# The second dense product of 23 token tiles by Strassen's seven half-size products, in a fused Fourier mixer and feed-forward kernel

## The chip, the cores and the metric

The kernel runs on one core of one Trainium2 chip. TensorE multiplies matrices and leaves the results in PSUM, in 8 banks of 512 f32 per partition; VectorE (DVE) and ScalarE (ACT) read PSUM and write SBUF; GpSimd (POOL) does some elementwise work and issues the DMAs of its own queue; SyncE (SP) issues the other DMAs. The metric is device time in microseconds, as the median of several runs.

## The reference

The input x has 8 batches of 3008 tokens by 256 features. First a Fourier mixer, then a feed-forward layer over all 24064 tokens:

```python
X = np.fft.rfft(x, axis=1)
Yr = Xr @ w_r - Xi @ w_i + b_r
Yi = Xr @ w_i + Xi @ w_r + b_i
# soft threshold of both at 0.01, then
y = np.fft.irfft(Y, n=3008, axis=1)

h = y @ w_in                  # 256 -> 2048
r = np.maximum(h, 0.0)
g = s * (r * r) + b
out = g @ w_out               # 2048 -> 256
```

The kernel computes in f16 with f32 sums. It multiplies r*r by w_out and applies s and b afterwards: out = s * (r*r @ w_out) + bias, where bias is b times the column sums of w_out.

## The kernel before

**Tiles and slots.** The feed-forward layer runs over 48 token tiles in a fixed order (`_tile_order`, L73): six "wide" tiles for each of batches 0 and 1 (512, 512 and 480 tokens, twice), then five "main" tiles of 512 for each later batch, and six "tail" tiles (512 or 384 tokens) made of the leftover tokens of two batches. The batches begin at tiles 0, 6, 12, 17, 23, 29, 35 and 41; the 384-token tails are tiles 28, 40 and 44. Each tile has 16 slots, one for each block `mc` of 128 hidden features. The main loop (L911 to L920) goes over tiles and slots. In slot `mc` of tile `ti` it writes down, in this order:

- the Fourier units that `plan` has for this slot,
- the first product of block `mc` of tile `ti` (`first_mm`, L768): two matmuls of up to 512 columns. They go to the two-bank PSUM tile `psh`, of which there are two. After each odd block one relu on ScalarE (L788) takes both banks to `rt` in SBUF (f32), and one square takes `rt` to `gt` (f16), on ScalarE (L792) or VectorE (L795). I call the squares of a tile k = 0 to 7; square k is written down in slot 2k + 1,
- a sixteenth of the second product of the tile before (`second_mms`, L837): for each of four groups of 128 tokens, 16 matmuls with a piece of `gt` as stationary operand and 256 columns of `w_out_t` as moving operand (L852), four per slot. Two groups share one PSUM bank (`psa`, two banks). After two groups one VectorE instruction (L862) applies s and the bias and writes `ost`, which SP stores.

**The Fourier units.** Batch 0 is transformed at the start (`first_batch`). The later ones go in small units spread over the slots of earlier tiles by `schedule` (L875 to L908): `s1_units` (a 94-point transform, whose result goes to DRAM and comes back in another layout), `s23_units` (the 32-point transform, the mixing, the threshold, the inverse transform, and DRAM again) and `s4_units` (the last 94-point transform, which writes `yt`). For a batch that begins at tile m, `s4_units` run in the last 14 slots before tile m, `s1_units` of the next batch end 8 slots before it, and `s23_units` of the next batch begin in its third slot.

**Who takes what.** `load` keeps a running sum of estimated microseconds for ScalarE and VectorE. PSUM evacuations (`evac`, L165) and the squares (L791) go to the engine with the lower sum; the fixed work of both engines is added where it is written down.

**Order in a queue.** The code only writes the instructions down. The framework under it puts each engine's instructions in an order of its own, by priority and by when it expects their inputs, and adds the waits for data and for buffers. A buffer pool with n buffers hands the same memory out again every n tiles, once all readers of the old tile are done.

Of the kernel before, what the change touches and what calls it, by code (L numbers as in the profile page):

```python
# [96 lines left out]
def kernel(  # L97
# [50 lines left out]
    dpool = ctx.enter_context(tc.tile_pool(name="dram", bufs=2, space=bass.MemoryType.DRAM))  # L148
    xpool = ctx.enter_context(tc.tile_pool(name="xp", bufs=4))
    upool = ctx.enter_context(tc.tile_pool(name="up", bufs=3))  # L150
    uspool = ctx.enter_context(tc.tile_pool(name="usp", bufs=5))
    xfpool = ctx.enter_context(tc.tile_pool(name="xfp", bufs=4))
    mpool = ctx.enter_context(tc.tile_pool(name="mp", bufs=2))
# [4 lines left out]
    rpool = ctx.enter_context(tc.tile_pool(name="rp", bufs=3))  # L158
    gpool = ctx.enter_context(tc.tile_pool(name="gp", bufs=15))
    opool = ctx.enter_context(tc.tile_pool(name="op", bufs=3))  # L160


    load = {"act": 0.0, "dve": 0.0}

    def evac(dst, src, cols, scale=None):  # L165
        ta, td = 0.17 + cols / 1200.0, 0.15 + cols / 960.0
        if load["act"] + ta <= load["dve"] + td:
            load["act"] += ta
            if scale is None:
                return None, nc.scalar.copy(out=dst, in_=src)  # L170
            return None, nc.scalar.mul(out=dst, in_=src, mul=scale)
        load["dve"] += td
        if scale is None:
            return nc.vector.tensor_copy(out=dst, in_=src), None
        return nc.vector.tensor_scalar_mul(out=dst, in0=src, scalar1=scale), None
# [24 lines left out]

    XCH = 8
    x16 = {}

    def emit_load_x(b, first=None):
        xv = x[b].rearrange("(n1 n2) d -> n1 (n2 d)", n2=N2)
        for c in range(N2 // XCH):
            t = xpool.tile([P, XCH * D], F16, name="x16", tag="x16")
            if first is not None:
                gate = nc.gpsimd.tensor_copy(out=t[0:1, 0:1], in_=first)
            parts = 2 if b == 0 else 1  # L210
            w = XCH * D // parts
            for i in range(parts):
                nc.gpsimd.dma_start(  # L213
                    out=t[0:N1, i * w : (i + 1) * w],
                    in_=xv[:, c * XCH * D + i * w : c * XCH * D + (i + 1) * w],
                )
            x16[(b, c)] = t
# [21 lines left out]

    b_g = cpool.tile([P, 2, D], F32, name="b_g")  # L240
    nc.vector.memset(b_g, 0.0)
# [4 lines left out]
    F_2 = [uspool.tile([P, H, P], F16, name="F_2", tag="us") for _ in range(2)]  # L246
    b_h = cpool.tile([P, D], F16, name="b_h")
    nc.vector.memset(b_h, 0.0)

    for i, bv in enumerate((b_r, b_i)):  # L250
        nc.gpsimd.dma_start(out=b_h[64 * i : 64 * i + 1], in_=bv.unsqueeze(0))
    sel_t = cpool.tile([P, P], F16, name="sel_t")
    eye_t = cpool.tile([P, P], F16, name="eye_t")
    C_t = cpool.tile([96, 96], F16, name="C_t")
# [83 lines left out]

    w_sum = cpool.tile([P, 2, D], F16, name="w_sum")

# [8 lines left out]
    def make_bias():  # L349
        ps = other_bank()  # L350
        for i in range(2):
            nc.tensor.matmul(ps[:, 0:D], ones, w_sum[:, i], start=(i == 0), stop=(i == 1))
        nc.scalar.activation(out=bias_bc, in_=ps[:, 0:D], func=AF.Copy, scale=bb_bc)

    us = {}
# [216 lines left out]
    def s1_units(b, more_banks=False):  # L572

        ud = dpool.tile([96, N2, D], F16, name="ud", tag="ud")
        hold = {}

        def unit(i):
            c, j = divmod(2 * i, XCH)
            if j == 0:
                hold["u"] = upool.tile([P, XCH, D], F16, name="u", tag="u")  # L580
            ps = any_bank() if more_banks else one_bank()
            nc.tensor.matmul(  # L582
                ps[0:96, :], A_t[0:N1, :], x16[(b, c)][0:N1, j * D : (j + 2) * D],
                start=True, stop=True,
            )
            u = hold["u"]
            evac(u[0:96, j : j + 2, :], ps[0:96, :].rearrange("p (j d) -> p j d", j=2), 512)
            if j == XCH - 2:
                nc.sync.dma_start(
                    out=ud[:, c * XCH : (c + 1) * XCH, :], in_=u[0:96]  # L590
                )
            if i == N2 // 2 - 1:
                uv = ud.rearrange("k n d -> (k n) d").rearrange("(q p) d -> p q d", p=P)
                for q in range(4):
                    t = uspool.tile([P, 6, D], F16, name="us", tag="us")
                    nc.sync.dma_start(out=t, in_=uv[:, 6 * q : 6 * q + 6, :])
                    us[(b, q)] = t

        return [lambda i=i: unit(i) for i in range(N2 // 2)]

    def s23_units(b):
# [8 lines left out]
        def fwd_unit(i):  # L610
# [13 lines left out]
            nc.vector.tensor_tensor(out=xt[:, 0], in0=xt[:, 1], in1=xt[:, 2], op=ALU.add)  # L624
            load["dve"] += 0.25
            xf[i] = xt

        def sum_unit(h):

            ps = one_bank().rearrange("p (i e) -> p i e", i=2)  # L630
            for i in range(2):
                for dc in range(DC):
                    nc.tensor.matmul(  # L633
                        ps[:, i, :], xf[2 * h + i][:, 0, dc], W_t[:, dc, 0],
                        start=(dc == 0), stop=(dc == DC - 1),
                    )
            s = mpool.tile([P, 2, D], F32, name="s", tag="m")
            nc.scalar.copy(out=s, in_=ps)
            load["act"] += 0.6
            hold[h] = s  # L640

        def mix_unit(i):
# [16 lines left out]
            nc.vector.tensor_tensor(out=t, in0=t, in1=m, op=ALU.subtract)  # L659
            load["dve"] += 1.75  # L660

# [53 lines left out]
    def s4_units(b):  # L715
# [6 lines left out]
        def unit(g):  # L722
# [5 lines left out]
            for j in range(w):  # L728
                h, k = divmod(n2 + j, HW)
                nc.tensor.matmul(  # L730
                    ps[:, j * 96 : (j + 1) * 96],
                    vs[(b, h)][:, k, ec * P : (ec + 1) * P], C_t,
                    start=True, stop=True,
                )
            evac(
                yt[:, ec, n2 : n2 + w, :],
                ps[:, 0 : w * 96].rearrange("p (j n) -> p j n", n=96), w * 96,
            )
# [27 lines left out]
    hold_h = {}  # L766

    def first_mm(ti, mc):  # L768
        tl = tiles[ti]
# [18 lines left out]
        nc.scalar.activation(out=rt[:, :, 0:w], in_=ps[:, :, 0:w], func=AF.Relu)  # L788
        gt = gpool.tile([P, 2, 512], F16, name="gt", tag="gt")
        load["act"] += 0.17 + w / 600.0  # L790
        if load["act"] + 0.25 + w / 600.0 < load["dve"]:  # L791
            nc.scalar.activation(out=gt[:, :, 0:w], in_=rt[:, :, 0:w], func=AF.Square)  # L792
            load["act"] += 0.25 + w / 600.0
        else:
            nc.vector.tensor_tensor(  # L795
                out=gt[:, :, 0:w], in0=rt[:, :, 0:w], in1=rt[:, :, 0:w], op=ALU.mult
            )
            load["dve"] += 0.15 + w / 480.0
        gts[(ti, mc // 2)] = gt

    def store(tl, sub, src):
# [35 lines left out]
    def second_mms(ti):  # L837

        tl = tiles[ti]
        w = width(tl)  # L840
        size = sub_size(tl)
        nsub = -(-w // size)
        hold = {}

        def mm(sub, mc):
# [3 lines left out]
            if h == 0 and mc == 0:  # L849
                hold["ps"] = other_bank().rearrange("p (h e) -> p h e", h=2)  # L850
            ps = hold["ps"]
            nc.tensor.matmul(  # L852
                ps[0:size, h, :], gts[(ti, mc // 2)][:, mc % 2, sub * size : (sub + 1) * size],
                w_out_t[:, mc, :],
                start=(mc == 0), stop=(mc == MC - 1),
            )
            if sub == nsub - 1 and mc % 2 == 1:
                gts.pop((ti, mc // 2))
            if mc == MC - 1 and (alone or h == 1 or sub == nsub - 1):
# [5 lines left out]
                )  # L865
                load["dve"] += 0.12 + 0.27 * k
                for i in range(k):
                    store(tl, sub - k + 1 + i, ost[:, i, :])

        return [lambda s=s, m=m: mm(s, m) for s in range(nsub) for m in range(MC)]  # L870


    plan = {}
# [10 lines left out]
    )  # L884
    load.update(act=0.0, dve=0.0)
    def load_x_2():
        emit_load_x(2, us[(1, 3)][0:1, 0, 0:1])

# [7 lines left out]
    plan.setdefault(14, []).append(make_bias)  # L896
    plan.setdefault(18, []).append(load_x_2)
    schedule(24, 42, s23_units(1))
    schedule(mark[1] - 12, 16, s4_units(1))
    for b in range(2, B):  # L900
# [6 lines left out]
        if b + 1 < B:  # L907
            plan.setdefault(s1 + 6, []).append(lambda b=b: emit_load_x(b + 1))  # L908

    ti_n = len(tiles)  # L910
    for ti in range(ti_n + 1):  # L911
        nxt = second_mms(ti - 1) if ti else []
        per_slot = -(-len(nxt) // MC)
        for mc in range(MC):
            if ti < ti_n:
                for u in plan.pop(ti * MC + mc, []):
                    u()
                first_mm(ti, mc)
            for u in nxt[mc * per_slot : (mc + 1) * per_slot]:
                u()  # L920
# [31 lines left out]
```

## Time and profile before

| what | before |
|---|---|
| median of 3 runs | 846.99 us (846.75 to 849.01) |
| span of the profiled execution, first to last instruction | 844.6 us |
| busy in the span: TensorE, its weight loads, VectorE, ScalarE | 835.1, 601.3, 694.7, 640.6 us |
| second product (L852): matmuls | 3024 |
| first product (L781): matmuls | 1536 |
| relu (L788), squares on VectorE (L795), squares on ScalarE (L792) | 384, 319, 65 |
| moved by DMA | 96.06 MB, 114 GB/s on average |

The median is of runs that were timed as a whole; the span is of one other execution, taken with the profiler, and counts from its first to its last instruction. Busy times are sums of instruction durations. Instructions on one engine overlap a little, matmuls much, so a busy share near 100% on TensorE does not yet say that it is at its peak pace; for that one looks at when consecutive matmuls start.

### The profile page before, as it was taken

The page shows a single profiled execution, that of the slowest core. Times are in us where ns is not written, and L with a number is a line of the kernel's source. Part 1 is how long each engine was busy: PE and PEld are TensorE (multiplying, and loading weights), DVE is VectorE, ACT ScalarE, POOL GpSimd, SP SyncE. Part 2 cuts the span into 40 slices and gives each one's busy share as a digit, 9 for nine tenths or more (in the row PEclk, how much of TensorE's full clock was granted, in tenths as well). Part 3 has the DMA queues.
Part 4 walks back from the last instruction along what each step waited for, and adds up shares of the span by engine and source line. Part 5 has one row for each costly group of instructions (what it writes and reads, how often), then busy time and mean ns, then how long its engine had stood idle before and what let it go on. Part 6 is the DMA issues. An engine that isn't in the chain of part 4 may idle for free.

```text
span 844.6 us, 17119 instructions
## 1 busy us (share of the span) xinstructions
PE 835.1 (99%) x6654; PEld 601.3 (71%) x6654; DVE 694.7 (82%) x1034; ACT 640.6 (76%) x862; POOL 45.9 (5%) x73
## 2 busy tenths in 40 slices
PE   8999999999999999999999999999999999999998
PEld 7857767777677766777677776777667777766765
DVE  5999987888888988888888888798978888776674
ACT  5987887778778877788777787778877778666673
POOL 4630000000000001000000000000000000000000
PEclk9999999999999999999999999999999999999999
DMA  7955467224851367324761247613354223411111
GB/s 200 181 151 118 119 161 199 74 77 98 202 156 54 103 171 188 93 70 107 189 174 50 81 101 196 172 43 90 106 152 125 59 78 97 113 33 38 38 44 50
DMA packets 105939, 96.06 MB, mean 114 GB/s; under 512 B 9607, under 2 KB 97675, under 8 KB 104515
## 3 DMA queue, kind: packets, MB, share of 16 engines
q1 hardware_dynamic: 99362, 80.55, 32.9%
q0 software_dynamic: 6496, 14.42, 10.6%
q8 instruction: 52, 0.85, 0.4%
q14 instruction: 29, 0.23, 0.1%
HBM read 53.52 MB, written 46.66 MB: 119 GB/s over the span
## 4 chain that ended last, share of the span: by engine, by line
PE 92%; ACT 3%; DVE 2%; DMA 1%; issue 1%; POOL 0%; DVEq 0%; ACTq 0%; POOLq 0%
PE psa L852 38%; PE psh L781 37%; PE psf L647 4%; PE psf L582 3%; PE psf L633 2%; PE psf L677 2%; PE psf L618 2%; PE psf L730 2%; ACT rt L788 1%; DMA x<-in_x_dram 1%; PE psm L425 1%; POOL x L213 0%; ACT yt L170 0%; DVE z L463 0%; PE psf L456 0%
## 5 line engine op out<-in xcount | busy, mean ns | idle before, releaser
L788 ACT ACTIVATE rt<-psh 128x1024 f32<-128x1024 f32 (+2 forms) x384 | 387.2, 1009 | 120.2 <-PE psh L781 118.8
L795 DVE TENSOR_TENSOR gt<-rt 128x1024 f16<-128x1024 f32 (+2 forms) x319 | 382.3, 1202 | 94.4 <-ACT rt L788 93.4
L852 PE MATMUL psa<-w_out_t,gt 128*128 128x256 f16 (+1 forms) x3024 | 454.4, 272 | 0.1
L852 PEld LDWEIGHTS <-gt 128*128 128x128 f16 (+1 forms) x3024 | 300.9, 101 | 186.6 <-issue 1.1
L781 PE MATMUL psh<-yt,w_in 128*128 128x512 f16 (+1 forms) x1344 | 396.8, 378 | 0.2 <-ACT rt L788 0.2
L781 PEld LDWEIGHTS <-w_in 128*128 128x128 f16 x1536 | 142.7, 98 | 26.2 <-issue 1.2
L862 DVE SCALAR_TENSOR_TENSOR ost<-psa,s_bc,bias_bc 128x512 f32<-128x512 f32 (+2 forms) x97 | 71.1, 733 | 9.6 <-PE psa L852 7.9
L792 ACT ACTIVATE gt<-rt 128x1024 f16<-128x1024 f32 (+2 forms) x65 | 68.2, 1050 | 0.9
L652 DVE TENSOR_TENSOR ring<-psf,s 128x512 f16<-128x512 f32 x84 | 57.6, 685 | 3.3 <-PE psf L647 3.2
L170 ACT CAST v<-psf 128x512 f16<-128x512 f32 x77 | 44.8, 582 | 19.4 <-PE psf L677 19.4
L170 ACT CAST xf<-psf 128x512 f16<-128x512 f32 x79 | 46.3, 586 | 8.8 <-PE psf L618 8.8
L781 PE MATMUL psh<-tail,w_in 128*128 128x512 f16 (+1 forms) x192 | 52.1, 353 | 0.0
L170 ACT CAST u<-psf 96x512 f16<-96x512 f32 x74 | 42.8, 580 | 11.2 <-PE psf L582 10.9
L647 PE MATMUL psf<-W_g,xf 128*128 128x256 f16 x336 | 50.4, 273 | 0.0
L170 ACT CAST yt<-psf 128x480 f16<-128x480 f32 (+2 forms) x76 | 39.0, 520 | 14.7 <-PE psf L730 14.2
L213 POOL DMA_DIRECT2D x<-in_x_dram x36 | 18.8, 527 | 432.9 <-PE psf L582 431.7
L582 PE MATMUL psf<-x,A_t 94*96 94x512 f16 x102 | 38.9, 382 | 1.0 <-ACT yt L170 0.6
L658 DVE TENSOR_TENSOR ring<-ring,high 128x512 f16<-128x512 f16 x84 | 35.6, 423 | 2.3
L659 DVE TENSOR_TENSOR ring<-ring 128x512 f16<-128x512 f16 x84 | 35.6, 423 | 2.1
L657 DVE TENSOR_TENSOR ring<-ring,low 128x512 f16<-128x512 f16 x84 | 35.5, 422 | 1.6
L647 PEld LDWEIGHTS <-xf 128*128 128x128 f16 x336 | 32.9, 98 | 4.1 <-issue 0.2
L730 PE MATMUL psf<-C_t,vs 96*128 96x96 f16 x448 | 33.2, 205 | 0.0
(100 smaller groups left out, 508.6 us busy)
## 6 DMA issues: line engine op xcount, KB each, us to landing
out_dram<-ost SPq DMA_DIRECT2D x152, 128.0 KB
ud<-u SPq DMA_DIRECT2D x28, 384.0 KB
us<-ud SPq DMA_DIRECT2D x28, 384.0 KB
vd<-v SPq DMA_DIRECT2D x42, 256.0 KB
vs<-vd SPq DMA_DIRECT2D x14, 768.0 KB
x<-in_x_dram POOLq DMA_DIRECT2D x28, 376.0 KB, 6.3
ring<-ring SPq DMA_DIRECT2D x280, 32.0 KB
out_dram<-ost SPq DMA_DIRECT2D x16, 120.0 KB
```

Source lines behind the costliest of these rows:

```text
L170: return None, nc.scalar.copy(out=dst, in_=src)
L582: nc.tensor.matmul(ps[0:96, :], A_t[0:N1, :], x16[(b, c)][0:N1, j * D : (j + 2) * D], start=True, stop=True,)
L647: nc.tensor.matmul(ps[:, r, :], xt[:, 2 - r, dc], W_g[:, dc, r], start=(dc == 0), stop=(dc == DC - 1),)
L652: nc.vector.tensor_tensor(out=t, in0=ps, in1=hold[i // 2][:, i % 2].unsqueeze(1).to_broadcast([P, 2, D]), op=ALU.add,)
L658: nc.vector.tensor_tensor(out=m, in0=m, in1=high, op=ALU.min)
L730: nc.tensor.matmul(ps[:, j * 96 : (j + 1) * 96], vs[(b, h)][:, k, ec * P : (ec + 1) * P], C_t, start=True, stop=True,)
L781: nc.tensor.matmul(o, w_in_t[dc][:, mc * P : (mc + 1) * P], r, start=(dc == 0), stop=(dc == DC - 1),)
L788: nc.scalar.activation(out=rt[:, :, 0:w], in_=ps[:, :, 0:w], func=AF.Relu)
L792: nc.scalar.activation(out=gt[:, :, 0:w], in_=rt[:, :, 0:w], func=AF.Square)
L795: nc.vector.tensor_tensor(out=gt[:, :, 0:w], in0=rt[:, :, 0:w], in1=rt[:, :, 0:w], op=ALU.mult)
L852: nc.tensor.matmul(ps[0:size, h, :], gts[(ti, mc // 2)][:, mc % 2, sub * size : (sub + 1) * size], w_out_t[:, mc, :], start=(mc == 0), sto ...
L862: nc.vector.scalar_tensor_tensor(out=ost[0:size, 0:k], in0=ps[0:size, 0:k], scalar=s_bc[0:size], in1=bias_bc[0:size].unsqueeze(1).to_broad ...
```

## The change

For 23 of the 48 tiles, `seven_mms` takes the place of `second_mms`. The 512 (or 480) tokens are cut in two halves i, the 16 hidden blocks into even and odd blocks k, and the 256 output columns into halves. With A(i,k) the squared activations and B(k,j) blocks of w_out, the product of 2 x 2 blocks is done with seven products of blocks instead of eight, by Winograd's form of Strassen's method: S1 = A21 + A22, S3 = A11 - A21, S2 = A11 - S1 (kept with the sign turned where that is handier), S4 = A12 + S2, and four combinations of w_out blocks (T), computed once on POOL. S1, S3 and S2 are f16 sums on VectorE, in two halves q each; S4 is a DMA from POOL's queue that adds A11 (by then S2) onto A12 in SBUF. A product n is for j in two token groups, 8 blocks c: matmuls of 128 columns. Two products share a bank, so a tile fills four groups of banks in turn, and `leave(group)` combines the finished products on VectorE with s and the bias.

`gt` becomes a larger tile that holds four squares of both halves (4 buffers of it instead of 15 of the small ones). The planner's prices are set anew: the fixed part of each (`over`) falls from 0.17 and 0.15 to 0.07 and 0.07 once the main loop begins, and the price of a relu and of both kinds of square likewise. The last 94-point transform computes 94 columns, not 96. To make room in SBUF, several pools change: x has 3 buffers and one apart (it was 4), `u` has 5 of half the size (3), `us` 4 (5), `xf` 3 (4), and small constants share memory with later tiles. The fourth chunk of each x is loaded later (slot 56 after the batch's start) than the other three.

The core of the diff:

```diff
@@ evac @@
+    over = {"act": 0.17, "dve": 0.15}
-        ta, td = 0.17 + cols / 1200.0, 0.15 + cols / 960.0
+        ta, td = over["act"] + cols / 1200.0, over["dve"] + cols / 960.0
@@ first_mm, after the relu @@
-        load["act"] += 0.17 + w / 600.0
-        if load["act"] + 0.25 + w / 600.0 < load["dve"]:
...
+        load["act"] += 0.07 + w / 600.0
+        if load["act"] + 0.09 + w / 600.0 <= load["dve"] + 0.07 + w / 480.0:
+            nc.scalar.activation(out=gt, in_=rr, func=AF.Square)
+            load["act"] += 0.09 + w / 600.0
         else:
...
+            load["dve"] += 0.07 + w / 480.0
@@ new: the block sums @@
+    def s_op(ti, n, q):
...
+        if n == 4:
+            nc.gpsimd.dma_start(out=a12, in_=a11, accum_op=ALU.add)
+            return
+        out, a, b, op = {
+            1: (s1, a21, a22, ALU.add),
+            3: (a21, a11, a21, ALU.subtract),
+            2: (a11, a11, s1, ALU.subtract),
+        }[n]
+        nc.vector.tensor_tensor(out=out, in0=a, in1=b, op=op)
+        load["dve"] += 0.07 + size / 480.0
@@ new: seven_mms @@
+        left = [(0, 0), (0, 1), (1, 1), None, (0, 0), (1, 0), (0, 1)]
+        right = [w_block(0, 0), w_block(1, 0), T[:, 3], T[:, 0], T[:, 1], T[:, 2], w_block(1, 1)]
+        def mm(n, j, c):
+            if n % 2 == 0 and j == 0 and c == 0:
+                hold[n // 2] = other_bank().rearrange("p (n j e) -> p n j e", n=2, j=2)
...
+        def leave(group):
...
+            if group == 0:
+                add(z[:, 0], bank(0), wide(bias_bc))
+                add(top[:, :, 0:P], bank(1), z[:, 0])
+                nc.vector.tensor_tensor(out=z[:, 1], in0=z[:, 0], in1=wide(b_21), op=ALU.add)
...
+            elif group == 1:
+                add(z[:, 0], bank(2), z[:, 0])
+                add(z[:, 1], bank(3), z[:, 1])
+            elif group == 2:
...
+                add(zs, two, zs)
...
+                for h in range(2):
+                    add(hold["o", 1][0:size, :, h * P : (h + 1) * P], bank(5), z[:, h])
...
+            else:
+                add(top[:, :, P:D], bank(6), z[:, 1])
...
+        C = MC // 2
+        order = [(n, j, c) for n in range(2) for j in range(2) for c in range(C - 1)]
+        order += [(n, j, C - 1) for n in range(2) for j in range(2)]
+        order += [(n, j, c) for n in range(2, 6) for j in range(2) for c in range(C)]
+        order += [(6, j, c) for h in range(2) for j in range(2) for c in range(4 * h, 4 * h + 4)]
+        slots = [[] for _ in range(MC)]
+        for at, what in enumerate(order):
+            slots[at // 7].append(lambda w=what: mm(*w))
+        for at, n, q in ((2, 1, 1), (3, 3, 1), (4, 2, 0), (5, 2, 1), (6, 4, 0), (6, 4, 1)):
+            slots[at].append(lambda n=n, q=q: s_op(ti, n, q))
+        for at, group in ((5, 0), (9, 1), (13, 2), (15, 3)):
+            slots[at].append(lambda group=group: leave(group))
@@ new: which tiles @@
+    def seven(ti):
+        if ti < 2 or ti >= len(tiles) - 1 or not halves(ti):
+            return False
+        firsts = [mark[b] // MC for b in range(1, B)]
+        return ti >= firsts[-1] or any(
+            m - 3 <= ti < m - 1 + (b > 1) for b, m in enumerate(firsts, 1)
+        )
@@ main loop @@
+            nxt = seven_mms(ti - 1) if seven(ti - 1) else second_mms(ti - 1)
...
                 first_mm(ti, mc)
+                if mc in (10, 11) and seven(ti):
+                    s_op(ti, 1 if mc == 10 else 3, 0)
```

`add(out, of, other)` is one VectorE instruction, of times s plus other; `halves(ti)` is true for tiles of 480 and 512 tokens. S1 and S3 of the first half are written down in slots 10 and 11 of the tile itself, everything else in the slots of the tile after it.

## The prediction

> **What bounds the kernel now.** I read the page first (busy shares and the costliest groups), then the chain of waits in a stretch with nothing but the two dense products, then the groups with their shapes kept apart, then timelines. The columns of a group are busy microseconds, mean nanoseconds of one, and idle time before them with its cause.
>
> ```profile
> PE 835.1 (99%) x6654; PEld 601.3 (71%) x6654; DVE 694.7 (82%) x1034; ACT 640.6 (76%) x862; POOL 45.9 (5%) x73
> ...
> L788 ACT ACTIVATE rt<-psh 128x1024 f32<-128x1024 f32 (+2 forms) x384 | 387.2, 1009 | 120.2 <-PE psh L781 118.8
> L795 DVE TENSOR_TENSOR gt<-rt 128x1024 f16<-128x1024 f32 (+2 forms) x319 | 382.3, 1202 | 94.4 <-ACT rt L788 93.4
> L852 PE MATMUL psa<-w_out_t,gt 128*128 128x256 f16 (+1 forms) x3024 | 454.4, 272 | 0.1
> ```
>
> TensorE is busy throughout and the second product's matmuls waited 0.1 us in all, while ScalarE's relu waited 118.8 us for TensorE and VectorE's square 93.4 us for the relu. The others wait for TensorE. A busy matmul row proves little, because rows overlap (272 ns is not the pace), so the pace comes from the chain (start, length, what):
>
> ```profile
> 759.39 0.43 PE psh L781 x2
> 759.82 0.44 PE psa L852 x4
> 760.26 0.43 PE psh L781 x2
> ```
>
> One slot is two first-product matmuls in 0.43 us and four second-product ones in 0.44, with nothing between: 216 ns for 512 columns, 109 ns for 256. Sixteen slots are 13.9 us, and a tile's second product is 64 x 109 ns = 6.98 us of it. Taking all matmul starts of the trace from the first tile on, gaps more than 60 ns over the pace sum to about 5.8 us, 0.12 us per tile. So a microsecond off TensorE's list is a microsecond off the time until another engine binds.
>
> **Part 1: seven half-size products.** A Strassen tile issues 7 x 2 x 8 = 112 matmuls of 128 columns instead of 64 of 256. Their price is the pace of 128-column matmuls that each load fresh weights. The forward transform of the first batch is such a run (timeline, TensorE alone):
>
> ```profile
> 23.31 0.22 PE L456 MATMUL psf<-g,F_t 128*128 128x128 f16 x1
> 23.37 0.22 PE L456 MATMUL psf<-g,F 128*128 128x128 f16 x1
> 23.43 0.22 PE L456 MATMUL psf<-g,F_t 128*128 128x128 f16 x1
> 23.48 0.22 PE L456 MATMUL psf<-g,F 128*128 128x128 f16 x1
> ```
>
> They start 56 ns apart though a weight load row reads 98 ns: loads overlap. 112 x 56 = 6.27 us, so a tile saves 0.70 us and its slot falls from 0.87 to 0.82 us. The rule in `seven` picks, by my count of the tile list, tiles 3, 4, 9-11, 14-16, 20-22, 26, 27, 32-34, 38, 39, 41-43, 45 and 46: 23 tiles. 23 x 0.70 = **16.2 us off TensorE**.
>
> [...] The trace has 56 in runs of nine, and I go by the trace.
>
> From the rows alone: the gain is gone if the pace is over 62 ns (16.2 us over 23 x 112 = 2,576 matmuls is 6.3 ns each). One of the 23 has 120-column weights, whose load reads 133 ns; at 256 columns its matmuls kept 109.
>
> **Part 2: the last transform at 94 columns instead of 96.** 448 matmuls at a 42 ns pace, 2 of 96 columns less: 0.9 ns each, **0.4 us off**.
>
> **Part 3: what VectorE gets.** Prices by shape:
>
> ```profile
> L862 DVE SCALAR_TENSOR_TENSOR ost<-psa,s_bc,bias_bc 128x512 f32<-128x512 f32 x84 | 62.7, 747 | 7.5 <-PE psa L852 5.9
> ...
> L658 DVE TENSOR_TENSOR ring<-ring,high 128x512 f16<-128x512 f16 x84 | 35.6, 423 | 2.3
> ...
> L624 DVE TENSOR_TENSOR xf<-xf 128x256 f16<-128x256 f16 x84 | 23.6, 286 | 6.4 <-ACT xf L170 6.1
> ...
> L862 DVE SCALAR_TENSOR_TENSOR ost<-psa,s_bc,bias_bc 128x256 f32<-128x256 f32 x5 | 2.4, 480 | 1.8 <-PE psa L852 1.8
> ```
>
> f16 sums cost 286 ns at 256 columns and 423 at 512, so 137 per 256: 697 ns at 1024. Six per tile (S1, S3, S2, two halves each) are 4.2 us. The outputs leave in seven 480 ns instructions, one of 747 and one f32 sum that lies between 286 and 480 (I take 400): 4.5 us, in place of 2 x 747 = 1.5. VectorE gets 7.2 us per tile, 166 us over 23, and could not hold it: 694.7 + 166 = 861. The planner moves squares instead. Its counters, worked through in the code's order with the new prices, leave 214 squares on VectorE (318 with the old ones; the page has 319): 105 go to ScalarE, -105 x 1.22 = -128 there and +105 x 1.06 = +112 here. VectorE ends near 733, ScalarE near 753: 89% of 2 x 833, from 79%. On average TensorE still binds. The tightest place is a stretch of dense work alone:
>
> ```profile
> core 0: us, PE busy (x) PEld busy (x) DVE busy (x) ACT busy (x) POOL busy (x), PEclk, DMA share, GB/s
> ...
> 753.10:767.00 13.90, 13.90 (x98) 9.40 (x97) 10.23 (x10) 9.20 (x10) 0.00 (x0) 1.00 0.16 48
> ```
>
> 19.4 us now; plus 7.2, less 0.16 for each of 3 or 4 squares that move, is 26.1 of 2 x 13.2 = 26.4. But rows of queued instructions overlap, like the 747 ns output in the next fence, whose successor starts 0.66 us after it: by starts I get about 0.09 us less per instruction, 23.4 us or 89%. That fits, with little room.
>
> **Part 4: new waits.** The order of an engine's queue decides what is late. It is not the order of the code:
>
> ```profile
> 759.86 1.03 ACT L788 ACTIVATE rt<-psh 128x1024 f32<-128x1024 f32 x1 [0.71 <-PE psh L781]
> ...
> 760.32 0.75 DVE L862 SCALAR_TENSOR_TENSOR ost<-psa,s_bc,bias_bc 128x512 f32<-128x512 f32 x1
> ...
> 760.98 1.22 DVE L795 TENSOR_TENSOR gt<-rt 128x1024 f16<-128x1024 f32 x1
> ```
>
> The code writes this square ahead of this output, yet the output ran first, while the relu was still running; so it was in 84 of 88 such pairs. The tool that builds the queues places an instruction where its inputs are expected. That matters at the bank hand-over. A Strassen tile fills four groups in two banks alternately, so the next tile's slot 0 needs the bank that `leave(2)` empties. Its matmuls end 0.88 us into slot 13, `leave(2)` needs 0.66 + 2 x 0.40 = 1.5 us, and slot 0 asks for the bank 3 x 0.82 + 0.43 = 2.9 us after slot 13 began: 0.5 us to spare if it is next in the queue. Likewise slot 0 wants the seventh square; relu and square end near 2.9 us and it is wanted at 3.2. Both are just in time, so small waits will come: at least 0, at most the 1.5 us of rival 1. I take 0.2 us per tile, somewhat more than the 0.12 that a tile shows now, because the engines are fuller: **4.6 us**.
>
> **The accumulating DMA** (S4) has no row; nearest is the load of x on the same queue, 376 KB against 256:
>
> ```profile
> DMA to landing us min/median/max: 4.3/6.4/11.3
> ```
>
> Two per tile, 0.52 us of POOL each, POOL being idle 95%. S2 should be done within slot 6, 5.8 us after slot 0; the issues fall at 5.8 and 6.3, the first readers at 11.4 (slot 13) and 12.3 (slot 14). Room is 5.6 us; landing takes 4.3 to 11.3 by the row. I take the low end, as the bytes are fewer and stay in SBUF: no wait. [...]
>
> **At nothing:** four f16 sums on POOL (by the 1.16 us row for 512 columns, some 2.3 us each), ready before tile 3's product; 28 more, smaller stores of u on SP, whose queue mostly waits for its data; one buffer fewer for x, u's loads and xf, each of whose next users is issued only after the last one's matmuls; the fourth chunk of x, issued when the first is consumed, 15 slots or more before use against a 6.4 us landing. Without that cover, x late by 1 us is 1 us of TensorE, six times at most.
>
> **Sum.** -16.2 - 0.4 + 4.6 = -12.0 us. The profiled span is 844.6, so 832.6; what lies around it to the median of 846.99 is 2.4: **835.0 us**.
>
> **Rivals.**
> 1. *Slower: the hand-over.* If `leave(2)` stands behind the square that the code writes before it, and the planner has that one on VectorE (20 of 23 tiles by its counters), then relu ends 1.7 us into slot 13, the square 2.9, `leave(2)` 4.4, against 2.9 wanted: 1.5 us x 20 = 30 us, 847.0 - 16.6 + 30 = 860. It decides from 0.72 us per tile on. For it: 7 us more VectorE work per tile just there; against it: the 84 of 88.
> 2. *No change: S4 lands late.* At the median of 6.4 us both are 0.8 us late at worst: 23 x 0.8 = 18 us, near 848. Against it: fewer bytes.
> 3. *Faster, but less: VectorE and ScalarE bind.* If rows overlap less than I think, a tile is paced by 26.1 us over two engines that are never split evenly, some 0.5 us over 13.2: 11.5 us, near 842.
> 4. *The narrow matmuls are slower* than 62 ns: slower than before. [...]
>
> **Chances.** Forecast 0.60, rival 1 0.16, rival 2 0.11, rival 3 0.11, rival 4 0.02. 0.3% is about what a measurement of this kernel can tell from no change. Faster 0.71, within 0.11, slower 0.18. The range takes the floor without waits (830.4, and a microsecond for fewer old gaps) to rival 2: 829.5 to 849.5, leaving out rivals 1 and 4.
>
> **What would show it.** New matmul rows 56 ns apart inside a slot; VectorE near 733 and ScalarE near 753; some 214 squares on VectorE. Rival 1: TensorE waiting for VectorE's output instructions at slot 0. Rival 2: TensorE's weight loads of `gt` waiting for a DMA in slots 13 and 14. Rival 3: first-product matmuls waiting for the relu. My forecast is wrong if TensorE's waits in the 23 tiles sum to over 16 us, or if the pace is not 56.

## The result and the profile after

| what | before | after |
|---|---|---|
| median | 846.87 us (846.58 to 849.01) | 892.50 us (884.47 to 895.14) |
| span of the profiled execution | 844.6 us | 892.6 us |
| mean granted TensorE clock in it | 0.998 | 0.981 |

The ratio is 1.052, with a 95% interval of 1.047 to 1.057: slower, where the prediction said 835.0 and a range up to 849.5. The median before is here over four executions (846.99 was over three). The floor of the prediction, the time before less all that the change takes off TensorE, is then 846.9 - 16.6 = 830.3. So 62.2 us have to be found.

The page of the changed kernel: busy time, share and instructions of each engine, the granted clock by slices, and the groups with busy time, mean of one in nanoseconds, and the idle time before them with its cause.

```profile
PE 835.3 (94%) x7758; PEld 606.6 (68%) x7758; DVE 732.8 (82%) x1238; ACT 730.3 (82%) x957; POOL 102.0 (11%) x123
...
PEclk9989998999999999999999999999999999999999
...
L839 ACT ACTIVATE rt<-psh 128x1024 f32<-128x1024 f32 (+2 forms) x384 | 385.9, 1006 | 73.1 <-PE psh L832 65.2
...
L852 DVE TENSOR_TENSOR gt<-rt 128x1024 f16<-128x1024 f32 (+2 forms) x218 | 268.2, 1233 | 59.9 <-ACT rt L839 58.8
...
L972 PE MATMUL psa<-w_out_t,gt 128*128 128x128 f16 (+1 forms) x1104 | 96.7, 225 | 30.1 <-DMA gt<-gt 28.5
L972 PE MATMUL psa<-T_s,gt 128*128 128x128 f16 (+1 forms) x1104 | 91.6, 219 | 0.0
```

VectorE's load came out as worked out (732.8 us, predicted 733; 218 squares, predicted 214), and neither it nor ScalarE is fuller than 82%. TensorE fell from 99% busy to 94%. The new matmuls (L972) that read T waited for nothing; the others, which read `gt` beside w_out and have the seventh product with its S4 among them, stood 28.5 us waiting for the accumulating DMA. The waits view (engine, line, cause: us in total, times, longest) shows how few waits that is:

```profile
PE psa L972 <- DMA gt<-gt: 28.5, 8, 5.1
```

Eight waits of up to 5.1 us, not 23 of 0.8. The view of the line that issues the DMA gives its landing time over 46 issues:

```profile
DMA to landing us min/median/max: 3.2/4.1/11.4
```

The median is what the prediction took (4.3 us). The maximum is what made the waits. All long waits are in the second product of the first Strassen tile of a group of tiles, seven times. This product is done in the slots of the next tile, so the waits lie in the slots of tiles 4, 10, 15, 21, 27, 33 and 39. Around one of them (slots of tile 33, timeline: start, length, engine, line, operation, count, idle time before):

```profile
653.08 0.86 POOL L943 DMA_DIRECT2D gt<-gt  x1 [19.98 <-PE psa L972]
654.59 1.11 SPq L723 DMA_DIRECT2D vs<-vd  x2
656.14 0.85 POOL L943 DMA_DIRECT2D gt<-gt  x1 [2.21 <-DVE zz L982]
...
661.86 0.50 PE L972 MATMUL psa<-w_out_t,gt 128*128 128x128 f16 x6
666.07 0.23 PE L972 MATMUL psa<-w_out_t,gt 128*128 128x128 f16 x1 [3.71 <-DMA gt<-gt]
...
667.18 1.91 PE L832 MATMUL psh<-tail,w_in 128*128 128x512 f16 x4
```

Between S4's two issues SP issues two loads of `vs`, 768 KB each. In the DMA packets of the trace these keep all 16 engines busy from 656.1 to 662, the last until 664.3 (8 KB packets of 515 ns each); none of S4's packets runs between 656.4 and 662, and the second S4, issued at 656.14, sends its first at 662.09. In all seven such tiles this first packet comes 5.5 to 7.3 us after the issue; in the others it comes after 1.4 to 1.5 us, in five of them after 2.0 to 3.5 (the 480-token tile is left out of this count). The seventh product then waits for it.

The last line shows what the wait brings behind it: four first-product matmuls in 1.91 us, 427 ns apart where 216 is the pace. A table by stretches (length, busy time and count of TensorE, granted clock, DMA share, GB/s) has the clock:

```profile
667.00:670.50 3.50, 3.50 (x27) 0.52 0.45 129
```

Six of the seven waits (3.1 to 5.1 us, in the slots of tiles 4, 10, 15, 21, 33 and 39) have a spell at half clock that begins between 1.5 us before their end and 1.5 us behind it, five of 3.4 us and one of 6.8; the shortest wait, 2.9 us in tile 27, has none. In the trace before, this happens once near the start and at the end; after, the six spells sum to 24 us, which is up to 12 us lost beside the 29.8 us for which, by the gaps between their starts, these matmuls waited.

The length of a wait alone does not decide this. In the traces of this case, past the first 40 us, all 11 waits of 3.7 us or more have such a spell, of the seven from 2.5 to 3.4 us four have one, and shorter ones have none. (A wait of 2.5 us in the version with banks grouped anew has one, a wait of 3.4 us in the version with T on VectorE has none.) What else decides it, no run shows.

The collision could be seen before. The same loads stand at the same place in the old kernel's trace (timeline of SP's queue; tile 33 begins there at 610.4):

```profile
616.10 0.80 SPq L693 DMA_DIRECT2D vs<-vd  x2
```

That is 5.7 us into the very tile in which S4's issues were expected at 5.8 and 6.3 us. The old trace shows the price as well: of the 20 loads of x that POOL issued after 90 us, all of 376 KB, the five that run beside two loads of `vs` landed in 8.5 to 10.7 us, the 15 others in 4.6 to 7.7.

A second loss is at the start. T, the four sums of w_out blocks, is computed on POOL while VectorE squares the first tiles (timeline):

```profile
50.65 5.19 POOL L366 TENSOR_TENSOR T_s<-w_out_t 128x1024 f16<-128x1024 f16 x2 [3.16 <-PE psa L613]
50.71 12.32 DVE L852 TENSOR_TENSOR gt<-rt 128x1024 f16<-128x1024 f32 x4 [1.36 <-ACT rt L839]
...
55.80 3.09 POOL L366 TENSOR_TENSOR T_s<-T_s,w_out_t 128x1024 f16<-128x1024 f16 x1
...
58.97 2.98 POOL L366 TENSOR_TENSOR T_s<-w_out_t,T_s 128x1024 f16<-128x1024 f16 x1
```

Four squares took 12.32 us, 3.08 each, where one costs 1.2 us elsewhere. The evacuation of `vs` stands behind these squares in VectorE's queue, and TensorE waits 4.6 us for it (and 2.6 us for relus that wait for buffers):

```profile
PE psf L520 <- DVE vs L178: 4.6, 1, 4.6
```

A spell of 6.8 us at half clock begins 0.5 us into this wait and lasts 2.7 us beyond it.

### The profile page after: what moved, and what is told of

The parts are those of the page before. It is cut to its first block, busy times and chain, and to the rows that moved or that the text cites. A ratio compares the mean times of both kernels' runs of the same rounds, so it can differ in the third digit from the quotient of the medians.

```text
span 892.6 us, 19903 instructions
## 1 busy us (share of the span) xinstructions
PE 835.3 (94%) x7758; PEld 606.6 (68%) x7758; DVE 732.8 (82%) x1238; ACT 730.3 (82%) x957; POOL 102.0 (11%) x123
## 4 chain that ended last, share of the span: by engine, by line
PE 64%; DVE 11%; DMA 10%; ACT 10%; issue 5%; POOL 0%; SPq 0%; DVEq 0%; ACTq 0%; POOLq 0%
PE psh L832 25%; PE psa L906 17%; DMA gt<-gt 8%; PE psa L972 8%; ACT rt L839 5%; DVE gt L852 4%; PE psf L677 3%; ACT gt L849 2%; PE psf L613 2%; PE psf L663 2%; PE psf L760 2%; PE psf L707 2%; PE psf L648 2%; DMA x<-in_x_dram 1%; DVE ost L982 1%
## 5 line engine op out<-in xcount | busy, mean ns | idle before, releaser
L852 DVE TENSOR_TENSOR gt<-rt 128x1024 f16<-128x1024 f32 (+2 forms) x218 | 268.2, 1233 | 59.9 <-ACT rt L839 58.8
L906 PE MATMUL psa<-w_out_t,gt 128*128 128x256 f16 (+1 forms) x1552 | 232.5, 273 | 4.2 <-DVE ost L982 4.1
L972 PEld LDWEIGHTS <-gt 128*128 128x128 f16 (+1 forms) x2208 | 153.3, 101 | 101.1 <-DMA gt<-gt 29.9
L849 ACT ACTIVATE gt<-rt 128x1024 f16<-128x1024 f32 (+2 forms) x166 | 173.6, 1045 | 3.4
L972 PE MATMUL psa<-w_out_t,gt 128*128 128x128 f16 (+1 forms) x1104 | 96.7, 225 | 30.1 <-DMA gt<-gt 28.5
L972 PE MATMUL psa<-T_s,gt 128*128 128x128 f16 (+1 forms) x1104 | 91.6, 219 | 0.0
L943 POOL DMA_DIRECT2D gt<-gt x46 | 40.6, 882 | 351.9 <-PE psa L972 146.5
L982 DVE SCALAR_TENSOR_TENSOR ost<-psa,s_bc,zz 128x256 f32<-128x256 f32 (+1 forms) x92 | 42.2, 479 | 25.7 <-PE psa L972 24.5
L221 POOL DMA_DIRECT2D x<-in_x_dram x36 | 19.8, 556 | 358.4 <-PE psf L613 355.2
L174 ACT CAST yt<-psf 128x470 f16<-128x470 f32 (+2 forms) x81 | 40.6, 510 | 6.9 <-PE psf L760 5.1
L174 ACT CAST xf<-psf 128x512 f16<-128x512 f32 x64 | 37.4, 585 | 6.3 <-PE psf L648 6.1
L982 DVE SCALAR_TENSOR_TENSOR zz<-psa,s_bc,zz 128x256 f32<-128x256 f32 (+3 forms) x69 | 37.3, 568 | 5.7 <-PE psa L972 5.4
```

The lines of the kernel that those rows point to most:

```text
L849: nc.scalar.activation(out=gt, in_=rr, func=AF.Square)
L852: nc.vector.tensor_tensor(out=gt, in0=rr, in1=rr, op=ALU.mult)
L906: nc.tensor.matmul(ps[0:size, h, :], lhs_of(ti, mc, sub), w_out_t[:, mc, :], start=(mc == 0), stop=(mc == MC - 1),)
L943: nc.gpsimd.dma_start(out=a12, in_=a11, accum_op=ALU.add)
L972: nc.tensor.matmul(hold[n // 2][0:size, n % 2, j], lhs, right[n][:, c], start=(n % 2 == 0 and j == 0 and c == 0), stop=(c == MC // 2 - 1), ...
L982: nc.vector.scalar_tensor_tensor(out=out, in0=of, scalar=s_bc[0:size], in1=other, op0=ALU.mult, op1=ALU.add)
```

## The experiments

Theory A: the loss is S4 behind the loads of `vs` in seven tiles, with the half clock that follows, plus the T sums on POOL, plus a remainder of small waits at tile borders and around the outputs. Rival B: VectorE and ScalarE are too full, so any version with the block sums stays slow. Rival C: the seven products themselves, the pools or the planner's new prices cost the time. All ratios are to the kernel before (846.55 to 847.11 us in these comparisons).

**S4 as a sum on VectorE, everywhere.**

```diff
-            nc.gpsimd.dma_start(out=a12, in_=a11, accum_op=ALU.add)
+            nc.vector.tensor_tensor(out=a12, in0=a12, in1=a11, op=ALU.add)
+            load["dve"] += 0.07 + size / 480.0
```

> S4 is computed by a VectorE sum (f16, 128x1024) in place of the accumulating DMA, two more such sums per Strassen tile, counted in the planner; all else as in the changed kernel. Theory A (the accumulating DMA of the first tile of each group stands behind the two 768 KB loads of vs, seven waits of 28.5 us in all, and each is followed by 3.4 us or more at half the clock): the waits for a DMA vanish and with them most of the half clock, some 39 us, so about 853 us. Theory B (VectorE and ScalarE are too full with Strassen, the DMA is only what ends last): 46 more sums of 0.69 us make VectorE fuller, no gain, 880 us or more. Theory C (the smaller pools and the new prices of the planner cost the time): no more than a few us of gain, 885 or more.

Measured: 856.96 us, 1.013 (1.010 to 1.017). 35.5 us gone (39 were expected), although VectorE has 46 more sums. B and C are out as the main cause.

**S4 left out.**

```diff
-            nc.gpsimd.dma_start(out=a12, in_=a11, accum_op=ALU.add)
```

> S4 is left out altogether (the seventh product takes A12 as it is, so the output is not the reference's); all else as in the changed kernel. Theory A: like the VectorE form, with 32 us less on VectorE: about 851 us. Theory B: VectorE and ScalarE have the same work as in the changed kernel, so 880 or more. If 851, the tile's other waits are small.

Measured: 853.01 us, 1.007 (1.005 to 1.009). The accumulating DMA with its consequences is worth 892.5 - 853.0 = 39.5 us. No matmul waits for `gt` from a DMA any more. The 2 us above the expected 851 are not explained.

**No Strassen tile, T sums kept on POOL.**

```diff
     def seven(ti):
+        return False
```

> No tile is a Strassen tile; the pools, the large gt tile, the prices, the 94 columns and the sums T on POOL stay. Theory A, with the T sums on POOL making the squares beside them last 3.1 us instead of 1.2 at the start (some 12 us): 847 + 10 to 12 = about 858 us. Theory B: the same, about 858. Theory C: the loss is mostly here, 870 us or more.

Measured: 855.08 us, 1.010 (1.007 to 1.013). With no second product done by Strassen's method it is still 8.5 us slower.

**The T sums on VectorE.**

```diff
-        nc.gpsimd.tensor_tensor(out=t[:, i], in0=a, in1=b, op=op)
+        nc.vector.tensor_tensor(out=t[:, i], in0=a, in1=b, op=op)
```

> The four T sums are done on VectorE instead of POOL; all else as in the changed kernel. Theory A: VectorE's squares at 50 to 63 us take 1.2 us again, TensorE's waits of 7.6 us and half clock of 6.8 us there go: about 880 us (12 us less than 892). If the slow squares were hidden or come from something else: 890 or more.

Measured: 880.25 us (875.03 to 884.19), 1.039 (1.033 to 1.044): 12.2 us gained, as expected, though both kernels' times spread over 9 to 11 us, so this figure is rough. The same place in its timeline:

```profile
49.38 2.36 DVE L852 TENSOR_TENSOR gt<-rt 128x1024 f16<-128x1024 f32 x2 [1.37 <-ACT rt L839]
51.66 0.69 DVE L366 TENSOR_TENSOR T_s<-w_out_t 128x1024 f16<-128x1024 f16 x1
52.26 3.49 DVE L852 TENSOR_TENSOR gt<-rt 128x1024 f16<-128x1024 f32 x3
```

A T sum costs VectorE 0.69 us, where POOL took about 3, and the squares around it are back at 1.2.

**Neither Strassen nor T sums, the rest of the change kept** (pools, planner's prices, 94 columns).

```diff
     def make_t(...):
-        nc.gpsimd.tensor_tensor(out=t[:, i], in0=a, in1=b, op=op)
+        return
     def seven(ti):
+        return False
```

> No Strassen tile, no T sums, everything else of the change (pools, large gt tile, prices, 94 columns). The run without Strassen tiles but with T on POOL took 855.1. If all of its loss is the T sums: 846.5, within 0.5 of before. If the pools cost something: 848 or more.

Measured: 846.67 us, 0.999 (0.998 to 1.000). All of the change but Strassen and T costs nothing that can be measured (the interval is 0.9 us to either side), so the T sums on POOL alone cost 855.1 - 846.7 = 8.4 us.

**Both remedies: S4 and T on VectorE.** The edits of the first and the fourth experiment together.

> S4 on VectorE in all 23 tiles and the T sums on VectorE. Theory A: the 857 us of the run with S4 on VectorE less the 10 us at the start, about 847 us, some us more than the form that keeps 16 tiles on the DMA, because VectorE has 32 us more work. Theory B in its weak form (VectorE's load costs nothing yet): the same as that form, within 2 us.

Measured: 849.24 us, 1.003 (1.002 to 1.004). 43.3 of the 62.2 us are back. Compared with S4 alone on VectorE, T's place gives 7.7 us. It was expected to be some us slower than the next version, in which VectorE has 32 us less to do; it is 2 us faster, which is about the noise of the two.

**S4 on VectorE only in the first tile of each group**, where the loads of `vs` are; the other 16 tiles keep the DMA. T on VectorE.

```diff
         if n == 4:
+            if any(ti == mark[b] // MC - 3 for b in range(1, B)):
+                nc.vector.tensor_tensor(out=a12, in0=a12, in1=a11, op=ALU.add)
+                load["dve"] += 0.07 + size / 480.0
+                return
```

> In the first tile of each group of Strassen tiles (seven tiles) S4 is a VectorE sum, in the 16 others it stays the accumulating DMA; the T sums are on VectorE. Theory A: both big terms are gone, 892 - 12 - 39 = about 842 us, and no TensorE wait for a DMA of gt is over 1 us. Theory D (the accumulating DMA is late in general, the first tile only shows it most): the waits move to the second tile of each group, 855 or more.

Measured: 851.36 us, 1.004 (1.003 to 1.006). Against the T sums' version alone, changing S4 in seven tiles gives 880.3 - 851.4 = 28.9 of the 31.0 us that changing all 23 gives: the place is settled. TensorE's waits for `gt` from a DMA are 1.3 us in all (one wait, in the slots of tile 5). The 842 that was expected was missed by 9; something else holds these 9.

**The loads of `vs` cut into pieces**, S4 left as a DMA in all tiles, T on VectorE. Each 768 KB load becomes four of 192 KB, with rows of 2 KB in place of 8.

```diff
-                    nc.sync.dma_start(
-                        out=t.rearrange("k n e -> k (n e)"),
-                        in_=vv[:, h * HW * D : (h + 1) * HW * D],
-                    )
+                    for c in range(4):
+                        nc.sync.dma_start(
+                            out=t[:, 4 * c : 4 * c + 4].rearrange("k n e -> k (n e)"),
+                            in_=vv[:, (h * HW + 4 * c) * D : (h * HW + 4 * c + 4) * D],
+                        )
```

> As the changed kernel with the T sums on VectorE (880 us), and each 768 KB load of vs is cut into four of 192 KB with rows of 2 KB instead of 8 KB; same bytes. If an engine of the 16 takes turns between the queues by packet, so that 8 KB packets of 0.51 us each hold S4's 2 KB ones up four times as long: S4's wait shrinks, some 850 to 865 us. If what is issued first is served first: no gain, 880.

Measured: 857.21 us, 1.012 (1.010 to 1.013), 23.0 us less than with whole loads. The waits view of the kernel with whole loads and T on VectorE, then of this one:

```profile
PE psa L972 <- DMA gt<-gt: 19.8, 7, 5.1
...
PE psa L973 <- DMA gt<-gt: 8.8, 5, 3.1
```

19.8 us of waiting became 8.8, with one spell of 3.4 us at half clock in place of 17 us. The second S4's first packet comes 1.6 to 5.1 us after its issue in the seven tiles (median 2.4), where with whole loads it was 2.0 to 7.2 (median 5.6). The longest wait that is left, 3.1 us, is in the slots of tile 5, where the last piece of `vs` was issued 7 us before. The bytes are the same; only the form of the loads changed. So most of the wait was for the `vs` loads, and their form sets its length. (Row size and number of loads changed together; which of the two it is was not tried.)

The kernel with whole loads and T on VectorE holds a test of its own: in tile 4 SP issued the loads of `vs` 2.9 us after the second S4 instead of 1.2 to 2.0 us before it, as in tiles 15, 21, 27, 33 and 39. There TensorE waited 0.3 us at most; in tile 10, where they came at the same time as the S4, 1.3; in those five 2.3 to 5.1.

In the slots of tile 33 of the changed kernel the two loads are 12 rows of 8 KB for each of 16 engines, which at 515 ns is 6.2 us, close to the 5.95 us that S4's first packet waited. How an engine chooses between the packets of two queues, no run here shows.

**All four block sums left out**, T on VectorE: VectorE has 120 us less to do.

```diff
     def s_op(ti, n, q):
...
-        nc.vector.tensor_tensor(out=out, in0=a, in1=b, op=op)
-        load["dve"] += 0.07 + size / 480.0
```

> All block sums S1, S2, S3 and S4 are left out on every engine (the seven products read the blocks as they are, so the output is not the reference's); matmuls, bank use and the output instructions stay; T sums on VectorE. VectorE has 120 us less than in the form with all sums on VectorE (849 us). Fullness theory (the 19 us of small TensorE waits there come from VectorE and ScalarE being at 87%): most go, about 833 us. Hand-over theory (they come from the output instructions' place in VectorE's queue and from waits at the tile borders): a good half stays, 840 us or more.

Measured: 839.74 us, 0.991 (0.990 to 0.993). This lies between the theories. Of the 18.9 us by which the version with both remedies stays above 830.3, 9.5 go with the sums, and 9.4 stay although VectorE has more time. The busy line shows that the planner used that time (83% and 83%, from 87 and 87):

```profile
PE 821.6 (98%) x7758; PEld 598.9 (72%) x7758; DVE 691.8 (83%) x1153; ACT 693.7 (83%) x908; POOL 55.5 (7%) x73
```

The traces say where both halves lie. Take, from the first tile on, what the time from one matmul's start to the next exceeds the pace of the first one's shape (median of that shape), if by more than 60 ns, and sort by what the second one waited for:

| gaps of TensorE, us | all | for an output instruction (`ost`) | of the Fourier units' matmuls | others |
|---|---|---|---|---|
| before | 5.0 | 0.0 | 3.9 | 1.0 |
| both remedies | 24.3 | 9.9 | 10.6 | 3.8 |
| the same without block sums | 14.7 | 7.6 | 5.8 | 1.3 |

The rows exceed the one of before by 19.3 and 9.7 us, which is the 18.9 and 9.4 within half a microsecond. Half of what goes with the block sums is in front of the Fourier units' matmuls; most of what stays is the wait for outputs. TensorE's waits with both remedies name no block sum, so what goes with the sums is VectorE's time and not a wait for their results. With both remedies there are 16 such waits of 0.15 to 1.3 us, all but one in the first slots of the next tile. In 14 of them (9.0 us), and in all 17 without the block sums, a square stands in VectorE's queue between the first and the last instruction of `leave(2)`.

**Banks grouped 1, 2, 2, 2** in place of 2, 2, 2, 1, so that the last output can begin earlier; otherwise as the version with S4 on VectorE in seven tiles.

```diff
-            if n % 2 == 0 and j == 0 and c == 0:
+            if n in (0, 1, 3, 5) and j == 0 and c == 0:
...
-        for at, group in ((5, 0), (9, 1), (13, 2), (15, 3)):
+        for at, group in ((4, 0), (7, 1), (11, 2), (15, 3)):
```

> As the form with the first tiles' S4 and the T sums on VectorE, and the seven products are spread over the four bank fillings as 1, 2, 2, 2 instead of 2, 2, 2, 1: the bank that slot 0 of the next tile needs is complete after product 5 of 7 (slot 11), not after product 6 (slot 13). Same matmuls and the same VectorE instructions less none. Hand-over theory (the rest above the floor is TensorE's wait for the output instructions at slot 0, some 6 to 9 us): 5 to 7 us less, about 836 us. If VectorE is simply full: no gain, 842.

Measured: 851.18 us, 1.006 (1.004 to 1.008), where 836 was expected: a miss. The plain tiles behind a group (18, 24, 36) are 1.1 us shorter than in the version with S4 on VectorE in seven tiles, so the hand-over is real there. But the waits only moved: by the gaps of TensorE those for an output instruction fell from 9.8 to 5.1 us, and 4.1 us of waits for the instructions of `leave` that write `zz` came instead. The profile of this version is of its longest execution (856.04 us), with a wait of 2.5 us for a load of `us` and half clock behind it, so its other tiles say little about the median.

**One square behind the outputs.** As the version with both remedies; in tiles where a plain second product follows a Strassen one, the square of slot 13 is written down behind the outputs of `leave(2)`.

```diff
+        if mc == 13 and ti and seven(ti - 1) and not seven(ti):
+            later.append(square)
...
+            while later:
+                with tc.issue_after(last_add[0].ins):
+                    later.pop()()
```

> As the form with S4 and T on VectorE everywhere (849.2 us), but in the nine tiles in which a Strassen product is followed by a plain one, the seventh square is written down after the three instructions of leave(2), with an order kept on VectorE. Hand-over theory: the 1.1 us wait at slot 0 of tiles 18 and 24 and smaller ones go, 845 to 846 us. If the wait only moves to the square's own reader: 849.

Measured: 847.49 us, 1.000 (0.999 to 1.001), 1.75 us better. The timeline at the border to tile 18, first without the edit:

```profile
351.86 0.75 DVE L983 SCALAR_TENSOR_TENSOR zz<-psa,s_bc,zz 128x512 f32<-128x512 f32 x1 [0.55 <-PE psa L973]
353.53 1.23 DVE L852 TENSOR_TENSOR gt<-rt 128x1024 f16<-128x1024 f32 x1 [0.92 <-ACT rt L839]
354.68 0.87 DVE L983 SCALAR_TENSOR_TENSOR ost<-psa,s_bc,zz 128x256 f32<-128x256 f32 x2
...
355.60 0.61 PE L906 MATMUL psa<-w_out_t,gt 128*128 128x256 f16 x4 [0.93 <-DVE ost L983]
```

and with it:

```profile
353.07 0.75 DVE L993 SCALAR_TENSOR_TENSOR zz<-psa,s_bc,zz 128x512 f32<-128x512 f32 x1 [0.54 <-PE psa L983]
...
354.33 0.87 DVE L993 SCALAR_TENSOR_TENSOR ost<-psa,s_bc,zz 128x256 f32<-128x256 f32 x2
...
355.71 0.60 PE L916 MATMUL psa<-w_out_t,gt 128*128 128x256 f16 x4
```

Without the edit, the queue puts the square between `leave(2)`'s first instruction and its outputs; VectorE idles 0.92 us for the relu, does the square, and only then empties the bank. This is rival 1's mechanism. Tiles 18 and 24 lost 1.1 us each by it and with the edit lose nothing. At both borders the planner then gave that square to ScalarE, so the run does not tell a later place in VectorE's queue from a place on the other engine; either way no square stands between them any more.

**Strassen in 11 tiles**: the first of each group, with S4 on VectorE, and tiles 41, 42, 43 and 45, with S4 by DMA; T on VectorE.

```diff
-        return ti >= firsts[-1] or any(
-            m - 3 <= ti < m - 1 + (b > 1) for b, m in enumerate(firsts, 1)
-        )
+        return firsts[-1] <= ti < len(tiles) - 2 or any(ti == m - 3 for m in firsts)
```

> Strassen only in the first tile of each group (seven tiles, S4 on VectorE) and in the last batch without tile 46 (four tiles, S4 by DMA), T sums on VectorE. By the spans of single tiles in the earlier runs these are the tiles that gained 0.3 to 0.7 us: about -5 us, 842 us. If a gain there only moves the wait to the following tile: 846.

Measured: 847.72 us, 1.001 (1.000 to 1.002), where 842 was expected: a miss. The first tiles of the groups gain 0.3 to 0.6 us each, and the tile behind each gives 0.2 to 0.75 back; of the four in the last batch two gain 0.3 and 0.5 and two nothing.

No version with Strassen products that computes everything came out faster than the kernel before; the best two are level with it.

## Why the prediction was wrong, point by point

- **What bounds the kernel**: right. TensorE bounds it, and a wait in front of a matmul reached the end of the kernel: by the gaps of TensorE 19.3 us more in the version with both remedies, 18.9 by its time.
- **Part 1, the pace**: right. Starts of the new matmuls are 56 ns apart (median of 2212 pairs), also with 120-column weights, and a tile without waits is 0.73 us shorter than before (0.70 predicted; tile 33 without block sums takes 14.70 us, before 15.43). Rival 4 is out.
- **Part 3, the loads of the engines**: VectorE came out right (732.8 for 733), ScalarE below the 753 predicted, at 730. That TensorE still binds on average holds; rival 3, first-product matmuls waiting for relus, appears nowhere in the dense work: first-product matmuls waited 2.7 us for relus in all, 2.6 of it beside the T sums.
- **S4**: "I take the low end, as the bytes are fewer and stay in SBUF: no wait" is the step that failed. As a price the value is right (4.1 us median landing, 4.3 taken). As a bound it isn't: in seven tiles the second S4 took 9.0 to 11.4 us, against a room of 5.6 (6.2 in tile 33). The row used for the price (4.3/6.4/11.3) had this in it: x loads beside the `vs` loads took 8.5 to 10.7 us, with the same bytes as the others. (Its maximum, 11.3, is another case: the last of four x loads in a row at the start.) The step never asked what else moves at that moment. Rival 2 named the place (slots 13 and 14) and the cause in general, and sized it as 0.8 us in every tile; it was 3 to 5 us in seven. Cost: 39.5 us, with the half clock that follows, against nothing predicted.
- **The half clock** was in no term. Of the seven waits for S4, six (3.1 to 5.1 us) brought 3.4 or 6.8 us at half clock, up to 12 us lost in all.
- **"At nothing"**: the T sums on POOL failed. The cover that was named hid T from its own readers, which did not wait. It did not hide POOL's work from VectorE, whose squares took 3.1 us beside it instead of 1.2. Cost: 7.7, 8.4 and 12.2 us in three pairs of kernels. The rest of that paragraph (pools, stores of `u`, fourth chunk of x) held: 846.67 with all of it kept.
- **Part 4, small waits**: "0.2 us per tile" is mis-sized. With S4 and T out of the way 849.24 - 830.3 = 18.9 us remain, 0.82 per Strassen tile. Where they lie was not foreseen either: in that version the first 22 tiles in whose slots a Strassen product runs are only 2.9 us shorter in sum, instead of 15.4, the tiles behind the groups 3.6 us longer and the others 1.1. About half (9.5 us) goes when VectorE is freed of the block sums, so the fullness that was weighed as "89% [...] with little room" did cost. Rival 1's mechanism is the larger part of the rest: a square between the instructions of `leave(2)` at 14 places, 0.3 to 1.3 us each and 9.0 us in sum, not 1.5 us at twenty. The "84 of 88" that spoke against it were counted in the kernel before, with one output at that place and not three. The edit that takes the square out of the way where a plain product follows gave 1.75 us.
- **What stays open**: the other 9.4 us persist with the block sums gone. By the gaps in that trace 7.6 us of them are waits for outputs, but no edit removed them all, so their cost is read and not shown by a run. Nor was it tried to move the `vs` loads to another slot.

The 62.2 us, then: 39.5 for S4 as a DMA, most of it behind the loads and with its half clock, some 8 for T on POOL, and some 15 of small waits (18.9 once S4 is VectorE's work too).

## What to carry to other kernels

A DMA put on a path with a deadline is judged by the landings in its worst company, not by its own bytes: look up in the trace which large transfers are issued within its window, and split the landing row by what ran beside each transfer (here 8.5 to 10.7 us beside the `vs` loads, 4.6 to 7.7 elsewhere). An operation given to an idle engine is free only if it does not slow a busy one (here VectorE's squares took 3.1 us instead of 1.2 beside POOL's sums), so check what the two would run side by side. A gain of 0.7 us per tile needs every border to have slack, and with VectorE and ScalarE at 87% it did not have it here.

## What the runs showed of the hardware

- An accumulating DMA of 256 KB within SBUF costs POOL 0.86 us to issue and lands in 3.2 us at best, 4.1 at the median, 11.4 behind 1.5 MB of loads with 8 KB rows. With those loads cut into pieces with rows of 2 KB TensorE's wait for it fell from 19.8 to 8.8 us.
- A 128 x 1024 f16 sum took 0.69 us on VectorE and 2.1 to 3.1 us on POOL next to VectorE's squares, which took 3.1 us instead of 1.2 meanwhile.
- Matmuls of 128 columns with a fresh weight load each started 56 ns apart (median of 2212 pairs), in runs of seven between wider ones.
- Past the first 40 us of the traces, with every wait of 3.7 us or more (11 of them), and with four of the seven from 2.5 to 3.4 us, TensorE ran at half clock for 3.4 or 6.8 us (427 ns for 512 columns instead of 216).
